# First layer of an attention and two-layer mixture-of-experts kernel: another split of the low-part work over VectorE and GpSimd, and another place for the score products

## The chip, the cores and the metric

One core of a Trainium2 chip runs the whole kernel. The metric is the device time of one execution in microseconds (us). Before the change the median of three runs is 1040.11 us (1038.76 to 1040.56). The profile is of one further execution of its own.

## What is computed

An attention with softmax over q's last axis and k's sequence axis (8 batches, 8 heads, 576 rows, 64 columns) gives 4608 tokens of 512 columns. Two expert layers follow. Each token goes to the one of 8 experts with the largest score; in layer 1 only tokens with a positive skip score are computed, the others pass through.

```python
for e in range(E):                       # layer 1, only where x @ w_skip > 0
    h = np.maximum(xc[mask] @ w1[e], 0.0)
    y[mask] = gate_w[mask, None] * (h @ w2[e])
out[do_compute] = xc + y
...
xn = x / norm(x); en = emb / norm(emb)   # layer 2, all tokens
expert_idx = argmax(xn @ en.T / tau)
out[mask] = gate_w[mask, None] * (np.maximum(x[mask] @ w1[e], 0.0) @ w2[e])
```

w1[e] is 512 x 1024, w2[e] is 1024 x 512.

## The kernel before

**High and low parts.** Every fp32 factor of a large product is used as a high part (rounded by ScalarE) and a low part (the rest), and a product is three matmuls: high by high, high by low, low by high. `hilo` (L513) makes the two parts of activations: ScalarE copies the high part out of PSUM, VectorE subtracts. `split` (L499) does the same for one expert's weights, w1 (r=0) or w2 (r=1), in 8 pieces of 128 x 512: `f` runs over 4 pairs of pieces, ScalarE writes each high part (L507), and VectorE or GpSimd writes the low part (L508), as the letter of the string `lo` says ('V' or 'P').

**Steps and blocks.** Tokens of a layer are sorted into areas by expert and worked in steps of up to two blocks of 128 tokens. A step with two blocks runs `L1two` (first product: 8 groups f of 12 matmuls, 256 tokens wide, two groups to one of the four PSUM tiles P4; after each odd f ScalarE applies the relu and VectorE takes h's low part, L541, L542), then `both` (transposes of the next step's tokens, the second of them into P4[0]), then `L2(1)` and, in the next call of `post`, `L2(0)` (second product, 24 matmuls of 512 columns each, block t into the PSUM tile py[t]). A step with one block runs `single` instead: `L1one` (24 matmuls and two relus), four groups of transposes (h in two halves, the next step's tokens in two), the four `hilo` of these, then `L2(0)`. In the run shown layer 1 has 17 steps, numbered 0 to 16; steps 2, 3, 8, 11 and 16 have one block, the other twelve two.

**Change of expert.** `change(k,r,lo)` is an `If` that splits weight r for step k where step k starts another expert, and then has SP load the expert after it (`reload`). In layer 1 steps 3, 4, 6, 9 and 12 start another expert; the w1 split stands in the `post` of the step before (letter C of the order string `seq`), the w2 split at the beginning of the step's own arm. All 8 low parts of each go to GpSimd ('PPPPPPPP').

**Layer 2's scores.** While layer 1 runs, the scores of its outputs for layer 2 are taken: `products(s,t,n)` multiplies block t of step s with the 8 rows of enB, the first n on VectorE (it reads the block's result out of py[t], L640), the other 8-n on GpSimd (it reads the copy in SBUF, L639) for ScalarE to add up (`sum`, L642). `mark`, `before` (four small matmuls) and `rank` make places of these and send the rows to the sorted X. Block 1 has all 8 products on VectorE, directly after `done(k,1)`; block 0 has 6 on VectorE and 2 on GpSimd, at the very beginning of the next step's `body` (`'pre': 'PV'`), ahead of `L1two` or `single`.

**Orders written by hand.** Each engine runs its instructions in the order of the program; nothing reorders them. `post(k)` runs L2(0) and then the letters of `seq` ('RGCMED': rank, gates, change of w1, mark, done and products of block 1, done of block 0), then gathers rows for step k+4. `body(k)` has `post(k-1)` and then the step's arm. The tail (`tail`) goes over to layer 2: it runs the first transposes of layer 2, the last `post`, the products of the last block, the w2 split, and then the first step of layer 2 in `begin`, with `one` (sum and mark) before group f1=4 of its `L1two` and `two` (total, rank, the plan's heads and rows, padding of X) before group f2=7.

**The start** (`start`): transposes of step 0, the count of tokens by expert (`total`), `split(0)` in the order VPVPVPVP with the plan's `heads` and `rows` between its pieces, padding of X and the load of enB by SP, `split(1)` in the order VPVPVPVP, then `begin`.

Of the kernel before, what the change touches and what calls it, by code (L numbers as in the profile page):

```python
# [472 lines left out]
class Moe:  # L473


    def __init__(self,tc,nc,sb,ps,cst,plan,raw,X,out,second,enD,accE,GE,ring,flags):
# [10 lines left out]
        self.enB,=st("enB",[128,8,512]); self.jk,self.ja=st("jk",[128,512],BF,2); self.pr=st("pr",[128,512],n=8-PRM["nd"])  # L487
# [11 lines left out]
    def split(self,r,mid=(),lo='VP'*4):  # L499

        nc=self.nc; H,L=self.hl[r]; n=0
        for f in range(4):
            if 0<f<=len(mid): mid[f-1]()
# [53 lines left out]
    def single(self,s):  # L557
# [78 lines left out]
    def products(self,s,t,n=8,eng='VP'):  # L636

        x=self.g(s)[:,t,0:512]
        for e in range(n,8) if 'P' in eng else (): self.nc.gpsimd.tensor_tensor(out=self.pr[e-n],in0=x,in1=self.enB[:,e],op=ALU.mult)  # L639
        for e in range(n) if 'V' in eng else (): self.nc.vector.scalar_tensor_tensor(out=self.jk,in0=self.py[t],scalar=1.0,in1=self.enB[:,e],op0=ALU.mult,op1=ALU.mult,accum_out=self.l2[s%2][:,t,e:e+1])  # L640
    def sum(self,s,t,n):
        for e in range(n,8): self.nc.scalar.activation(out=self.ja,in_=self.pr[e-n],func=AF.Copy,accum_out=self.l2[s%2][:,t,e:e+1])  # L642
# [70 lines left out]
    def layer(self,first,ws,after,kmin,gdeps=()):  # L713
# [8 lines left out]
        def change(k,r,lo='VP'*4):  # L722
            if k>=NST: return
            with tc.If(self.val(1,k)>0):  # L724
                self.split(r,(),lo)
                reload(k,r)
        def start():
            self.fresh()
            if first:
# [8 lines left out]
                with c.Else(): plan.rest(first); self.late(first,ws)  # L738
# [6 lines left out]
            self.done(0,0,first); self.val(3,1)  # L745
        def body(k):
# [7 lines left out]
            def sum():  # L754
                if first: self.sum(k-1,0,PRM['nd'])
            F=dict(P=lambda: self.products(k-1,0,PRM['nd'],'P'),V=lambda: self.products(k-1,0,PRM['nd'],'V'),M=lambda: self.mark(k-1),S=sum)
# [3 lines left out]
            if not B['chg']: change(k,1,B['lo'][0])  # L760
# [11 lines left out]
        def post(k):  # L772
# [11 lines left out]
            F=dict(C=lambda: change(k+1,0,B['lo'][2]),M=lambda: self.mark(k-1),S=lambda: self.sum(k-1,0,PRM['nd']),R=R,G=G,E=D1,D=lambda: self.done(k,0,first))  # L784
            for x in B['seq']: F[x]()
            gather(k+4)
            if k%2 and k+1<NST and not first: self.sums(k+1,2)
        def tail(k):
            if not first: post(k-1); return
# [3 lines left out]
            def one(): self.sum(k-1,0,n); self.mark(k-1)  # L793
# [6 lines left out]
            with tc.If(self.early(False,ALL)>0) as c:  # L800
                self.both(0,self.P4[1]); post(k-1); self.products(k-1,0,n); self.split(1,(),PRM['lot'])
                self.begin(False,{PRM['f1']:one,PRM['f2']:two},two if PRM['f2']==8 else None)
            with c.Else():
                post(k-1); self.split(1); self.products(k-1,0,n); one(); two(); plan.rest(False); self.late(False,after)
# [15 lines left out]
PRM={'nt': 6, 'lot': 'PPPPPPPP', 'f0': 6, 'f1': 4, 'f2': 7, 'nd': 6, 'sum': 6, 'bef': 5, 'chg': 1, 'lo': ['PPPPPPPP', 'PPPPPPPP', 'PPPPPPPP'], 'pre': 'PV', 'seq': 'RGCMED', 'early': 6, 'step': 14.514, 'win': 0.1, 'fine': {0: 2, 7: 2, 3: 2, 2: 2, 4: 2, 1: 2, 5: 2, 6: 2}, 'bufs': {'eq': 3, 'ek': 2, 'kt': 2, 'qt': 2, 'vp': 3, 'vt': 2, 'xb': 2}, 'kV': (1, 3, 7), 'qV': (), 'nA': (2, 3, 5), 'off': {'k': -12.612, 'v': 53.868, 'q': 30.476, 'K': 5.621, 'O': 26.55, 'S': 50.0}, 'tail': (6, 7), 'ob': {'v5': -85.388, 'v7': -18.189, 'q3': 3.525, 'S4': -39.842, 'v4': 49.0, 'k2': -20.193, 'v0': -57.765, 'q7': 7.453, 'k1': -50.913, 'q2': -16.574, 'K4': -7.68, 'O0': -28.323, 'v1': -80.086, 'k0': -78.46, 'q6': -32.531, 'S5': -23.128, 'K0': -77.087, 'v2': 43.27, 'K7': 21.272, 'S2': -15.874, 'k4': 14.156, 'K6': -16.911, 'v6': 32.148, 'O7': 57.371, 'S7': -5.118, 'O6': 53.378, 'K5': -39.633, 'S3': -23.995, 'q1': -13.481, 'S0': 2.649, 'O2': -14.143, 'k7': 29.483, 'q0': -9.813, 'S6': 18.001, 'q4': -35.591, 'S1': -22.407, 'k3': 2.681, 'K3': -62.071, 'O4': 17.684, 'k5': 10.878, 'q5': 2.694, 'K1': -34.335, 'O5': 18.815, 'K2': -14.953, 'v3': 36.47, 'k6': 37.121, 'O1': -10.351, 'O3': -3.795}}  # L820
# [41 lines left out]
```

## Time and profile before

| | us |
|---|---|
| median of the runs | 1040.11 |
| profiled execution, own time | 1045.66 |
| its span, first to last instruction | 1043.9 |
| attention (first matmul of layer 1 at) | 0 to 171.6 |
| layer 1, first matmul of step 0 to first matmul of layer 2 | 171.6 to 565.05 |
| layer 2, to the end of the span | 565.05 to 1043.9 |
| PE busy, share of the span | 92% |
| DVE, ACT, POOL busy | 57%, 44%, 39% |

PE is TensorE's matmul queue, DVE VectorE, ACT ScalarE, POOL GpSimd, SP the queue that issues most transfers. A timeline row has start, duration, engine, line and operation, output and inputs, shape, and in brackets the idle time before it with what released it. Matmuls overlap, so the distance of two starts tells more than a duration.

### The profile page before, as it was taken

Reading aid. Unit: us, or ns where it says so; the run is one execution under the profiler, and the core shown is the slowest. Engines: PE = TensorE matmul, PEld = TensorE weight load, DVE = VectorE, ACT = ScalarE, POOL = GpSimd, SP = SyncE. Lnnn points to the kernel's source line nnn. Section 1 sums busy time; section 2 is a strip of 40 time slices with the busy share of each in tenths; the row PEclk is TensorE's granted clock in tenths of the full one; section 3 lists DMA queues with packets and bytes.
Section 4 is the critical chain, followed back from the end, with each engine's and each line's share of the span. In section 5 each row is a group of like instructions: output and inputs, shape, how many; then the busy total and the mean of one; then the engine's idle time right before and its main releaser. Section 6 shows DMA issues by size and latency. Waiting matters only on the chain. (4 is left out here: it accounts for less than half of the span.)

```text
span 1043.9 us, 19789 instructions
## 1 busy us (share of the span) xinstructions
PE 958.6 (92%) x6075; PEld 854.5 (82%) x6075; DVE 593.0 (57%) x1576; ACT 458.8 (44%) x914; POOL 410.3 (39%) x363
## 2 busy tenths in 40 slices
PE   2988996898899999999998899999999999999994
PEld 2988885785799887779987799889898899998893
DVE  5788987874477766757775522361723423255371
ACT  5787734136343261432225423353625332455352
POOL 5487747109937174291125600041402300134040
PEclk9999997998999999999998899999999999999997
DMA  9998646634525224252111381061432610063400
GB/s 297 327 316 285 205 158 220 221 111 164 206 74 204 64 82 167 81 178 86 44 45 46 137 273 60 22 235 33 153 110 79 216 43 22 22 220 119 169 32 22
DMA packets 88632, 144.72 MB, mean 139 GB/s; under 512 B 23439, under 2 KB 48015, under 8 KB 88288
## 3 DMA queue, kind: packets, MB, share of 16 engines
q1 hardware_dynamic: 78528, 115.42, 33.8%
q0 software_dynamic: 8640, 26.61, 6.8%
q8 instruction: 74, 1.21, 0.5%
q14 instruction: 142, 1.16, 0.4%
q10 hardware_dynamic: 1248, 0.32, 0.1%
HBM read 111.08 MB, written 33.68 MB: 139 GB/s over the span
## 5 line engine op out<-in xcount | busy, mean ns | idle before, releaser
L538 PE MATMUL P<-xT,w1h 128*128 128x256 f32 x1856 | 341.6, 286 | 5.5 <-ACTq L724 2.2
L568 PE MATMUL py<-w2h,hT 128*128 128x512 f32 x1072 | 344.8, 397 | 0.3
L538 PEld LDWEIGHTS P<-xT,w1h 128*128 128x128 f32 x1856 | 294.8, 194 | 8.7 <-issue 4.2
L538 PE MATMUL P<-xT,w1l 128*128 128x256 f32 x928 | 266.0, 287 | 4.5 <-POOL w1l L508 4.2
L568 PEld LDWEIGHTS py<-w2h,hT 128*128 128x128 f32 x1072 | 202.6, 190 | 45.6 <-DVE hT L515 3.7
L568 PE MATMUL py<-w2l,hT 128*128 128x512 f32 x536 | 212.3, 396 | 4.6 <-POOL w2l L508 3.5
L542 DVE SCALAR_TENSOR_TENSOR hT<-P,hT 128x512 fp32r<-128x512 f32 x116 | 77.5, 687 | 210.2 <-ACT hT L541 210.1
L538 PEld LDWEIGHTS P<-xT,w1l 128*128 128x128 f32 x928 | 180.3, 194 | 6.3 <-POOL w1l L508 5.5
L580 POOL DMA_INDIRECT out_dram<-y,idt x38 | 38.6, 1017 | 286.5 <-ACT y L579 234.9
L640 DVE SCALAR_TENSOR_TENSOR jk<-py,enB 128x512 bf16<-128x512 f32 x198 | 136.9, 691 | 24.3 <-ACT xb L576 10.7
L541 ACT ACTIVATE hT<-P 128x512 fp32r<-128x512 f32 x116 | 67.9, 596 | 171.1 <-PE P L538 167.9
L568 PEld LDWEIGHTS py<-w2l,hT 128*128 128x128 f32 x536 | 101.5, 189 | 32.7 <-POOL w2l L508 11.2
L508 POOL TENSOR_TENSOR w1l<-kt,w1h 128x512 fp32r<-128x512 f32 x64 | 84.3, 1351 | 64.4 <-ACT w1h L507 64.2
L508 POOL TENSOR_TENSOR w2l<-vt,w2h 128x512 fp32r<-128x512 f32 x76 | 103.1, 1386 | 1.3 <-issue 0.7
L579 ACT ACTIVATE y<-py,gate 128x512 f32<-128x512 f32 x38 | 26.0, 688 | 117.5 <-PE py L568 111.3
L507 ACT CAST w2h<-vt 128x512 fp32r<-128x512 f32 x104 | 55.5, 616 | 5.8 <-issue 4.3
L507 ACT CAST w1h<-kt 128x512 fp32r<-128x512 f32 x104 | 55.7, 636 | 0.5 <-DMA xb<-X 0.5
L576 ACT COPY xb<-py 128x512 f32<-128x512 f32 x17 | 10.0, 587 | 96.3 <-DVE flag L651 50.0
L515 DVE TENSOR_TENSOR hT<-P,hT 128x512 fp32r<-128x512 f32 x18 | 12.4, 686 | 64.7 <-ACT hT L514 64.7
L639 POOL TENSOR_TENSOR pr<-xb,enB 128x512 f32<-128x512 f32 x20 | 25.4, 1291 | 60.0 <-ACT xb L576 60.0
L550 PE MATMUL P<-w1h,xT 128*128 128x512 f32 x144 | 48.2, 407 | 0.7 <-issue 0.7
L220 PE MATMUL p<-vp,ek 128*128 128x130 f32 x320 | 43.9, 291 | 3.5 <-ACT ek L210 2.6
(243 smaller groups left out, 1301.3 us busy)
## 6 DMA issues: line engine op xcount, KB each, us to landing
vt<-in_moe_w_dram SPq DMA_DIRECT2D x26, 1024.0 KB
kt<-in_moe_w_dram SPq DMA_DIRECT2D x26, 1024.0 KB
xb<-X SPq DMA_DIRECT2D x56, 266.0 KB
kt<-in_k_dram SPq DMA_DIRECT2D x16, 512.0 KB
vt<-in_v_dram SPq DMA_DIRECT2D x16, 512.0 KB
qt<-in_q_dram SPq DMA_DIRECT2D x8, 1024.0 KB
xg<-X SPq DMA_DIRECT2D x28, 266.0 KB
X<-empty SPq DMA_DIRECT2D x16, 266.0 KB
```

The source lines that it names most:

```text
L220: for j in range(NS): T.matmul(o,lhsT=ek.tile[:,j,2*c:2*c+2].rearrange(hd),rhs=vp.tile[:,2*c:2*c+2,j],start=j==0,stop=j==NB)
L507: nc.scalar.copy(h,a)
L508: (nc.gpsimd if lo[2*f+i]=='P' else nc.vector).tensor_tensor(out=l,in0=a,in1=h.bitcast(F32),op=ALU.subtract)
L538: T.matmul(o,lhsT=w[:,c,128*f:128*f+128],rhs=x[:,c],start=n==0,stop=n==11); n+=1
L541: A.activation(out=h,in_=q,func=AF.Relu)
L542: V.scalar_tensor_tensor(out=hl[:,f-1:f+1],in0=q,scalar=0.0,in1=h.bitcast(F32),op0=ALU.max,op1=ALU.subtract)
L550: T.matmul(self.P4[f],lhsT=x[:,c,0:128],rhs=w[:,c,512*f:512*f+512],start=n==0,stop=n==11); n+=1
L568: T.matmul(self.py[t],lhsT=x[:,c,a],rhs=w[:,c],start=n==0,stop=n==23); n+=1
L579: A.activation(out=y,in_=p,func=AF.Copy,scale=gt)
L580: P.indirect_dma_start(out=self.out,out_offset=IO(self.idt[:,i:i+1]),in_=y,in_offset=None,bounds_check=NTOK-1,oob_is_err=False)
L639: for e in range(n,8) if 'P' in eng else (): self.nc.gpsimd.tensor_tensor(out=self.pr[e-n],in0=x,in1=self.enB[:,e],op=ALU.mult)
L640: for e in range(n) if 'V' in eng else (): self.nc.vector.scalar_tensor_tensor(out=self.jk,in0=self.py[t],scalar=1.0,in1=self.enB[:,e],op0 ...
```

## The change

In layer 1 the low parts of w1 at a change of expert go to VectorE (all 8), those of w2 stay on GpSimd. At the start all of w1's go to VectorE, with the plan's heads and rows behind them, and all of w2's to GpSimd, in two halves: pairs 0 and 1 ahead of `begin`, pairs 2 and 3 inside its first product. Both blocks now have 6 products on VectorE and 2 on GpSimd (four tiles `pr` in place of two). GpSimd's follow the w2 split; ScalarE's sums of both blocks stand behind `both`. VectorE's products of block 0 move from ahead of the first product to behind the first low part of h in `L1two`; in a step of one block they, `before` and the sums move from ahead of `single` to behind it. In such a step the w2 split is made in halves, pairs 0 and 1 ahead of `single`, pairs 2 and 3 between its second and third `hilo`. The last `post` has another order ('GCRMED'), keeps w1 on GpSimd and all 8 products on VectorE; `one` moves to group 1 and `two` behind the first product.

```diff
-    def split(self,r,mid=(),lo='VP'*4):
+    def split(self,r,lo='VP'*4,part=range(4)):
...
-        for f in range(4):
-            if 0<f<=len(mid): mid[f-1]()
+        for f in part:
...
-        h(); x(); g(); y()
+        h(); x(); mid(); g(); y()
...
-        for e in range(n,8) if 'P' in eng else (): self.nc.gpsimd.tensor_tensor(out=self.pr[e-n],in0=x,in1=self.enB[:,e],op=ALU.mult)
+        for e in range(n,8) if 'P' in eng else (): self.nc.gpsimd.tensor_tensor(out=self.pr[(8-n)*t+e-n],in0=x,in1=self.enB[:,e],op=ALU.mult)
...
-                self.split(0,(lambda: plan.heads(cst['base0'][:,0:8]),lambda: plan.rows(8*AREA,0,5)))
+                self.split(0,'V'*8); plan.heads(cst['base0'][:,0:8]); plan.rows(8*AREA,0,5)
...
-                self.split(1)
-                with tc.If(early>0) as c: self.begin(first)
+                def w2(*f): return lambda: self.split(1,'P'*8,f)
+                w2(0,1)()
+                with tc.If(early>0) as c: self.begin(first,{2:w2(2),4:w2(3)})
...
-                if first: self.products(0,1)
+                if first: self.products(0,1,PRM['nd'],'V')
...
-            if first:
-                for x in B['pre']: F[x]()
-            def arm(c): return lambda: [x() for w,x in ((B['sum'],sum),(B['bef'],before)) if w==c]
+            def P():
+                if first: [self.products(k-1,t,PRM['nd'],'P') for t in range(2)]
+            def V():
+                if first: self.products(k-1,0,PRM['nd'],'V')
+            def arm(c): return lambda: [x() for w,x in ((2,V),(B['sum'],sum),(B['bef'],before)) if w==c]
             with tc.If(two>0) as c:
                 if B['chg']: change(k,1,B['lo'][0])
+                P()
                 self.L1two({f:arm(f) for f in range(8)})
                 self.both(k+1,self.P4[0])
                 arm(8)()
                 self.L2(1)
             with c.Else():
-                if B['chg']: change(k,1,B['lo'][1])
-                for f in range(8): arm(f)()
-                self.single(k)
-                arm(8)()
+                change(k,1,B['lo'][1],(0,1))
+                self.single(k,lambda: change(k,1,B['lo'][1],(2,3)))
+                P()
+                for f in range(9): arm(f)()
...
+            nd,seq,lo=(PRM['nt'],PRM['seqt'],PRM['lot']) if last and first else (PRM['nd'],B['seq'],B['lo'][2])
...
-                    if first: self.products(k,1)
+                    if first: self.products(k,1,nd,'V')
...
-                self.both(0,self.P4[1]); post(k-1); self.products(k-1,0,n); self.split(1,(),PRM['lot'])
+                self.both(0,self.P4[1]); post(k-1,True); self.products(k-1,1,n,'P'); self.products(k-1,0,n); self.split(1,PRM['lot'])
```

In the table of constants of layer 1: `nt` 6 to 8, `seqt` 'GCRMED' (new), `f1` 4 to 1, `f2` 7 to 8, `sum` 6 to 8, the third string of `lo` 'PPPPPPPP' to 'VVVVVVVV'; `'pre': 'PV'` is gone.

## Rows read from the trace of the kernel before

**Rows 1.** Stretches of 25 us: length, busy PE, PEld, DVE, ACT, POOL, clock, DMA.

```profile
225.00:250.00 25.00, 21.34 (x91) 16.55 (x91) 15.22 (x47) 14.89 (x31) 16.54 (x14) 0.86 0.16 50
...
325.00:350.00 25.00, 25.00 (x170) 23.02 (x169) 18.14 (x54) 7.24 (x18) 11.30 (x10) 1.00 0.46 158
```

**Rows 2.** Timeline of PE, first matmul of steps 3 to 6, 8 to 10.

```profile
238.59 0.47 PE L550 MATMUL P<-w1h,xT 128*128 128x512 f32 x1
...
261.32 0.47 PE L538 MATMUL P<-xT,w1h 128*128 128x256 f32 x2 [0.16 <-issue]
...
291.49 0.40 PE L538 MATMUL P<-xT,w1h 128*128 128x256 f32 x2
...
315.17 0.40 PE L538 MATMUL P<-xT,w1h 128*128 128x256 f32 x2
...
362.80 0.47 PE L550 MATMUL P<-w1h,xT 128*128 128x512 f32 x1
...
377.10 0.40 PE L538 MATMUL P<-xT,w1h 128*128 128x256 f32 x2
...
405.45 0.40 PE L538 MATMUL P<-xT,w1h 128*128 128x256 f32 x2
```

**Rows 3.** Timeline of PE, first matmul of step 3 that reads a low part.

```profile
241.81 0.79 PE L550 MATMUL P<-w1l,xT 128*128 128x512 f32 x1 [2.74 <-POOL w1l L508]
```

**Rows 4.** Waits of the whole span: who for whom, us in total, times, longest.

```profile
PEld py L568 <- POOL w2l L508: 11.2, 17, 0.7
```

**Rows 5.** Stretches behind waits of PE: length, busy PE, PE clock, DMA share, GB/s.

```profile
241.80:247.70 5.90, 5.89 (x14) 0.51 0.00 0
...
556.00:561.60 5.60, 5.58 (x17) 0.50 0.00 1
...
264.20:268.00 3.80, 3.80 (x18) 0.56 0.70 257
...
577.40:582.00 4.60, 4.58 (x30) 0.64 0.10 40
...
198.40:200.40 2.00, 0.01 (x1) 1.00 0.85 244
```

**Rows 6.** Timeline of PE, transposes and second product of step 2.

```profile
229.60 0.60 PE L527 MATMUL pxT<-ident,xb 128*128 128x128 f32 x4
...
231.05 0.66 PE L555 MATMUL P<-ident,h 128*128 128x128 f32 x4 [0.85 <-ACT h L551]
...
232.38 0.50 PE L568 MATMUL py<-w2h,hT 128*128 128x512 f32 x1
```

**Rows 7.** Timeline of DVE: step 2's last low part; six products, first and last.

```profile
234.24 0.68 DVE L515 TENSOR_TENSOR xT<-P,xT 128x512 fp32r<-128x512 f32 x1
...
239.91 0.69 DVE L640 SCALAR_TENSOR_TENSOR jk<-py,enB 128x512 bf16<-128x512 f32 x1 [0.65 <-ACT xb L576]
...
243.58 0.69 DVE L640 SCALAR_TENSOR_TENSOR jk<-py,enB 128x512 bf16<-128x512 f32 x1
```

**Rows 8.** Timeline of PE, second transposes of the first step.

```profile
186.83 0.66 PE L527 MATMUL P<-ident,GE 128*128 128x128 f32 x4 [0.92 <-DVE hT L542]
```

**Rows 9.** Timeline of PE, change of layers: transposes, layer 2's first product, count.

```profile
556.02 1.09 PE L527 MATMUL pxT<-ident,GE 128*128 128x128 f32 x4 [4.16 <-issue]
...
565.05 0.40 PE L538 MATMUL P<-xT,w1h 128*128 128x256 f32 x2
...
577.41 0.17 PE L496 MATMUL pm<-oh,ones 128*1 128x8 bf16 x1 [2.14 <-DVE oh L670]
```

**Rows 10.** Timeline of ACT, eight high parts of w2 in step 9.

```profile
379.21 4.26 ACT L507 CAST w2h<-vt 128x512 fp32r<-128x512 f32 x8 [0.53 <-issue]
```

**Rows 11.** Low parts of weights, L508: min/median/max ns, first and last start.

```profile
L508 POOL TENSOR_TENSOR w2l<-vt,w2h x76: 1251/1286/1778, 177.7 to 1013.4; 128x512 fp32r<-128x512 f32 x76
...
L508 DVE TENSOR_TENSOR w1l<-kt,w1h x40: 669/683/1790, 171.7 to 1002.2; 128x512 fp32r<-128x512 f32 x40
```

**Rows 12.** ACT's sums of GpSimd's products, L642: min/median/max ns.

```profile
L642 ACT ACTIVATE jk<-pr x34: 622/630/632, 209.8 to 575.2; 128x512 bf16<-128x512 f32 x34
```

More of the change, by code (lines that the diff above doesn't have):

```diff
@@ L498, in total @@
         self.nc.vector.tensor_copy(self.plan.cnt,p)
[L499 to L503 removed]
+    def split(self,r,lo='VP'*4,part=range(4)):
+        nc=self.nc; H,L=self.hl[r]
+        for f in part:
             for i in range(2):
@@ L556, in Th, with single @@
         return lambda: self.hilo(p,*[t[:,4*g:4*g+4,0:128] for t in self.hT])
-    def single(self,s):
+    def single(self,s,mid):
         self.L1one()
         x,h,y,g=self.Tx(s+1,0),self.Th(0),self.Tx(s+1,1,self.P4[0]),self.Th(1)
-        h(); x(); g(); y()
+        h(); x(); mid(); g(); y()
     def L2(self,t,mid=None):
@@ L721, in reload, with change @@
                     with tc.If(nx<9): self.load(r,after[r],0)
-        def change(k,r,lo='VP'*4):
+        def change(k,r,lo='VP'*4,part=range(4)):
             if k>=NST: return
             with tc.If(self.val(1,k)>0):
-                self.split(r,(),lo)
-                reload(k,r)
+                self.split(r,lo,part)
+                if part[-1]==3: reload(k,r)
         def start():
@@ L732, in start @@
                 self.total(self.accE)
-                self.split(0,(lambda: plan.heads(cst['base0'][:,0:8]),lambda: plan.rows(8*AREA,0,5)))
+                self.split(0,'V'*8); plan.heads(cst['base0'][:,0:8]); plan.rows(8*AREA,0,5)
                 self.arrange(first,gdeps)
                 nc.sync.dma_start(out=self.enB.rearrange('p e d -> p (e d)'),in_=self.enD.rearrange('e d -> (e d)').unsqueeze(0).to_broadcast([128,4096]))
-                self.split(1)
-                with tc.If(early>0) as c: self.begin(first)
-                with c.Else(): plan.rest(first); self.late(first,ws)
+                def w2(*f): return lambda: self.split(1,'P'*8,f)
+                w2(0,1)()
+                with tc.If(early>0) as c: self.begin(first,{2:w2(2),4:w2(3)})
+                with c.Else(): w2(2,3)(); plan.rest(first); self.late(first,ws)
             for s in (2,3,4): gather(s)
@@ L743, in start, with sums @@
                 self.done(0,1,first)
-                if first: self.products(0,1)
+                if first: self.products(0,1,PRM['nd'],'V')
             self.done(0,0,first); self.val(3,1)
+        def sums(k,n):
+            for t in range(2): self.sum(k,t,n)
         def body(k):
@@ L754, in sum @@
             def sum():
-                if first: self.sum(k-1,0,PRM['nd'])
-            F=dict(P=lambda: self.products(k-1,0,PRM['nd'],'P'),V=lambda: self.products(k-1,0,PRM['nd'],'V'),M=lambda: self.mark(k-1),S=sum)
-            if first:
-                for x in B['pre']: F[x]()
-            def arm(c): return lambda: [x() for w,x in ((B['sum'],sum),(B['bef'],before)) if w==c]
-            if not B['chg']: change(k,1,B['lo'][0])
+                if first: sums(k-1,PRM['nd'])
+            def P():
[3 more added lines that the diff above has]
+            def arm(c): return lambda: [x() for w,x in ((2,V),(B['sum'],sum),(B['bef'],before)) if w==c]
             with tc.If(two>0) as c:
                 if B['chg']: change(k,1,B['lo'][0])
+                P()
                 self.L1two({f:arm(f) for f in range(8)})
@@ L783, in G @@
                 if k%2==0: self.gates(k,2,first)
-            F=dict(C=lambda: change(k+1,0,B['lo'][2]),M=lambda: self.mark(k-1),S=lambda: self.sum(k-1,0,PRM['nd']),R=R,G=G,E=D1,D=lambda: self.done(k,0,first))
-            for x in B['seq']: F[x]()
+            F=dict(C=lambda: change(k+1,0,lo),M=lambda: self.mark(k-1),R=R,G=G,E=D1,D=lambda: self.done(k,0,first))
+            for x in seq: F[x]()
             gather(k+4)
@@ L788, in tail @@
         def tail(k):
-            if not first: post(k-1); return
+            if not first: post(k-1,True); return
             if k==0:
@@ L792, in tail, with one @@
             n=PRM['nt']
-            def one(): self.sum(k-1,0,n); self.mark(k-1)
+            def one(): sums(k-1,n); self.mark(k-1)
             def two():
@@ L800, in tail @@
             with tc.If(self.early(False,ALL)>0) as c:
-                self.both(0,self.P4[1]); post(k-1); self.products(k-1,0,n); self.split(1,(),PRM['lot'])
+                self.both(0,self.P4[1]); post(k-1,True); self.products(k-1,1,n,'P'); self.products(k-1,0,n); self.split(1,PRM['lot'])
                 self.begin(False,{PRM['f1']:one,PRM['f2']:two},two if PRM['f2']==8 else None)
             with c.Else():
-                post(k-1); self.split(1); self.products(k-1,0,n); one(); two(); plan.rest(False); self.late(False,after)
+                post(k-1,True); self.split(1); self.products(k-1,1,n,'P'); self.products(k-1,0,n); one(); two(); plan.rest(False); self.late(False,after)
         twos={}
```

8 lines of the change are left out of this document (4 added, 4 removed).

## The prediction

> **What bounds the kernel now.** I read first the stretches of 25 us, then the timeline of TensorE by steps, then what ended its waits. In most of layer 1 TensorE is the bound: a quiet stretch has it busy for all of its 25.0 us at full clock, while one with steps of one block and changes of expert shows 21.3 us and a clock of 0.86 [rows 1]. So the steps are compared by their first matmuls. A plain step of two blocks lasts 315.17 - 291.49 = 23.7 us, step 8 (one block) 14.3, step 9 (another expert) 28.4, step 4 (another expert) 30.2, step 3 (one block, another expert) 22.7 [rows 2]. Steps 11 and 12 repeat 8 and 9 within 0.1 us. What is above 23.7 in steps 4, 9 and 12 is 6.5 + 4.7 + 4.7 us, and its releaser is GpSimd, which makes w1's eight low parts and only then w2's: step 3 waits 2.74 us for w1's [rows 3], the second products wait in 17 pieces for w2's [rows 4]. Behind four of TensorE's waits the granted clock stands at 0.51, 0.50, 0.56 and 0.64 for 5.9, 5.6, 3.8 and 4.6 us, near the lower of its two levels (1.2 of 2.4 GHz); one idle stretch of 2.0 us stands at 1.00 [rows 5]. Lost behind the four are (1 - clock) x length: 2.9, 2.8, 1.7 and 1.7 us, 2.3 in the mean.
>
> **Steps of one block: the products get in front of the second product.** In step 2 the transposes start at 229.60 and the second product at 232.38, 2.8 us later, 0.85 of it a wait for ScalarE [rows 6]. VectorE's six products of the block before are over by then, since they stand ahead of `single`. In the new order they stand behind its last low part. They read py[0] in PSUM, and the second product, L2(0), is the next thing to write py[0]: it has to wait for the last of them. VectorE ends the last low part at 234.24 + 0.68 = 234.9 [rows 7], about 0.9 earlier if ScalarE's wait goes with the sums, so 4.4 us behind the start of the transposes. Six products take 243.58 + 0.69 + 0.08 - 239.91 = 4.4 us [rows 7]. With 0.2 us to TensorE the second product starts 9.0 us behind the transposes in place of 2.8: +6.2 us, an idle time of over 6 us. A wait of TensorE for VectorE to leave a PSUM tile does occur in the old trace (0.92 us for P4[0] [rows 8]); for py it does not, since the products were always early. I add 2.3 us for the clock (bounds 0 and 2.9 [rows 5]): **+8.5 us** in each of steps 2, 8 and 11, +25.5.
>
> Step 16 has the same order, but there TensorE waits 4.16 us at the change of layers anyway [rows 9], and the products run beside it: 0 (without that cover +8.5).
>
> Step 3 also splits w2. Its second half puts four copies on ScalarE (half of 4.26 us [rows 10]) ahead of h's second half, so the products end about 2 us later: two products of TensorE (14.3 - 2.8 = 11.5), a gap of 11.0, and 2.3 for the clock give 24.8 in place of 22.7: **+2.1**. The stall on w1 that it has today is saved in this.
>
> **Changes of expert.** VectorE takes 0.68 us for a low part at the median where GpSimd takes about 1.29 [rows 11]: eight in 5.4 us, while L2(0) of a step of one block, with its slow clock, lasts some 8. GpSimd is then free for w2 as soon as ScalarE has copied: 8 x 1.29 = 10.3 us within the first product (about half of a step's 23.7). Steps 4, 9 and 12 come down to a plain 23.7: **-15.9** (upper bound: all that they have above it; lower: 0, if another queue is late).
>
> Step 6 follows a step of two blocks and pays today nothing for its change. In the new order VectorE does rank, eight low parts and `mark` ahead of done of block 1. ScalarE starts w1's copies behind four sums (0.63 each and a read of the accumulator, some 3.3 us [rows 12]), so the low parts end about 10 us behind the start of step 5's second product. Then come on VectorE and ScalarE `mark` 1.4, done of block 1 0.8, its copy 0.6, six products 4.4, done of block 0 0.8, its copy 0.6 (estimates from such pieces of step 5): 18.6, that is 7.6 behind the 11.0 of the second product. ScalarE's copies of w2 (4.3 [rows 10]) are queued ahead of the relus, so h's first low part is there at 7.6 + 4.3 + 1.4 = 13.3 of step 6, where the transposes into P4[0] want it at 12.1: 1.2 us. Another 4.4 us of products and 0.7 later comes its second low part, at 18.4, where the second product, begun at 13.9, wants it at 15.6: some 2.7 us. With 1.7 for the clock [rows 5]: **+5.6** (bounds 0 and 7).
>
> **Start and change of layers.** At the start VectorE is rid of w2's low parts, so the 0.92 us wait goes: **-0.9** [rows 8]. The plan's heads now follow eight low parts, so SP's eight paddings and the load of enB come some 6 us later; the first products may wait for enB, with VectorE's room ahead of `both` as cover: 0 (without it up to +2). SP's gathers still wait for the plan's later rows, as now. At the change of layers `mark` no longer waits for GpSimd's products behind w1's split. The 2.14 us [rows 9] go, and the 1.7 us of slow clock behind them [rows 5]: **-3.8**. The count then stands behind the first product, where TensorE has the transposes to do, and the scatters on GpSimd come no later than now.
>
> **At nothing:** two more products on GpSimd and two sums on ScalarE in each plain step (2.6 and 1.6 us), beside an idle GpSimd and behind `both`; without that cover `mark` comes some 0.3 us late. VectorE is relieved of 1.5 us a step that never reached TensorE. The second `If` for w2 in steps without a change and the loads of weights on SP: 0 to +1 in all. Layer 2 keeps its orders.
>
> **Sum:** 25.5 + 2.1 - 15.9 + 5.6 - 0.9 - 3.8 = +12.6 us. The profiled execution took 1045.66 us, 5.6 above the median of the runs (1040.11), and would take 1058.3; on the median it is **1052.7 us**.
>
> **Rivals.**
> - *Faster: the products do not hold L2(0).* VectorE is idle between done of the block before and the low parts of h. If the products run in that time, as they do today, every gap stays closed. Then steps 2, 8 and 11 lose even the 0.85 wait [rows 6] (-2.6), step 3 comes to about 17 us under GpSimd's pace (-5.7), and with -15.9, -0.9 and -3.8 and no backlog in step 6 it is -28.9: 1011 us. It decides where the second product of step 2 starts under 4 us behind its transposes. Against it: the program's order on VectorE. Chance 0.07.
> - *No change: the clock holds.* The gaps come, but cost no half speed: 4 x 2.3 + 1.7 less, and a little less in step 6: about 1041. For it: the idle stretch at 1.00. Against it: the four others [rows 5]. Chance 0.12.
> - *Slower still: VectorE's split is slowed by GpSimd.* Old low parts of w1 on VectorE run up to 1.79 us where GpSimd subtracts beside them [rows 11]. At 1.1 us, an estimate between median and maximum, each split is 3.4 us longer; what of it TensorE sees lies between 0 and 5 x 3.4, and I take half, 8.5: 1061 us. Against it: GpSimd has no subtractions at most of these times. Chance 0.13. The Trainium skill (GPSIMD Engine Reference, section 1, Specifications) says that GpSimd's way to SBUF contends with VectorE instructions that have two SBUF inputs; the low parts are such, the products and h's low parts, with an input in PSUM, are not. By that rule the trace agrees: 0.68 alone, 1.79 at worst beside GpSimd.
>
> **Numbers.** The forecast has 0.64, its own range 1045 to 1060; 0.04 is left for what I don't see. A measurement of this kernel can tell about 0.2%, 2.1 us, from no change. The case of the holding clock reaches from 1035 to 1046 and gives 0.05 to faster, 0.04 to the same, 0.03 to slower; the unheld products give 0.07 to faster; the forecast gives 0.02 to the same and 0.62 to slower, the slowed split 0.13 to slower, the unknown 0.01, 0.02 and 0.01. The range from 1040 to 1063 leaves out the unheld products, the lower part of the holding clock and the worst of the slowed split.
>
> **What would show it.** Right: in steps 2, 3, 8 and 11 the first matmul of py stands 9 to 11 us behind the transposes, released by VectorE's products, with a clock near 0.5 behind it; steps 4, 9, 12 at 23.7; w1's low parts on VectorE near 0.68 us; a wait of 2 to 3 us in step 6's second product; no wait of the count. The forecast is wrong if those gaps are under 3 us, if the clock stays at 1.00 behind them, or if steps 4, 9 and 12 keep over 2 us of their excess.

## The result, and the profile after

The changed kernel takes 1051.26 us (median of four runs, 1050.05 to 1051.72); the kernel before takes 1040.34 beside it (four runs, 1038.76 to 1041.74). The ratio is 1.0104, 95% interval 1.0086 to 1.0121: slower by 10.9 us, where 12.6 was forecast. The profiled execution took 1051.72, its span is 1050.0.

The two spans can't be subtracted as they stand: the attention, which the change does not touch, ended 6.1 us earlier in the second one (first matmul of step 0 at 165.53, before at 171.60). From that matmul to the end it is 884.5 us, before 872.3: +12.2. The steps show where it lies. Each number is the distance of two first matmuls in the timeline of TensorE; the columns behind "after" are the experiments A to I below, and row 17 is layer 2's first step.

```
step     before  after    A      B      C      D      E      F      G      H      I
2         14.52  22.37  13.62  19.65  22.04  22.04  22.04  13.63  13.58  13.57  13.57
3         22.73  24.04  24.38  23.89  24.40  23.87  23.84  24.57  18.44  23.36  18.93
4         30.17  23.67  28.15  25.25  24.16  23.68  23.67  26.35  31.83  23.77  29.02
6         23.66  29.10  30.42  29.10  24.28  29.06  27.90  24.19  25.42  25.42  27.67
8         14.30  22.48  14.50  19.66  21.53  22.43  21.34  15.61  16.82  16.88  16.88
9         28.35  23.66  26.30  23.93  23.66  23.65  23.66  24.66  23.66  23.67  23.66
11        14.25  21.91  16.69  19.87  21.35  21.85  21.30  15.88  16.28  17.75  17.62
12        28.36  23.67  24.04  23.65  23.67  23.65  23.65  23.84  24.01  23.65  23.66
16        21.71  21.94  19.01  21.32  21.70  21.96  21.67  19.30  19.31  20.76  19.77
17        30.31  30.83  30.97  30.66  30.01  36.07  31.25  29.27  31.54  30.68  30.41
```

Timeline of TensorE in the changed kernel: transposes, second product and next step of step 2 (rows 6 and 2 before), the second product of step 3, the two waits of step 6, and layer 2's second step.

```profile
222.34 0.60 PE L526 MATMUL pxT<-ident,xb 128*128 128x128 f32 x4
...
231.01 0.76 PE L567 MATMUL py<-w2h,hT 128*128 128x512 f32 x1 [6.50 <-DVE cl L686]
...
239.27 0.39 PE L549 MATMUL P<-w1h,xT 128*128 128x512 f32 x1
...
255.16 0.76 PE L567 MATMUL py<-w2h,hT 128*128 128x512 f32 x1 [8.28 <-DVE cl L686]
...
325.67 1.12 PE L526 MATMUL P<-ident,xb 128*128 128x128 f32 x4 [2.54 <-DVE hT L541]
...
330.55 0.50 PE L567 MATMUL py<-w2h,hT 128*128 128x512 f32 x1 [0.84 <-DVE hT L541]
...
602.61 0.80 PE L537 MATMUL P<-xT,w1h 128*128 128x256 f32 x2 [6.57 <-ACTq L723]
```

In step 2 the second product now starts 8.7 us behind the transposes, 6.5 of them idle; before it was 2.8 [rows 6]. The last row is the wait that nobody forecast; it stood at 2.2 before. Its releaser, ACTq L723, is ScalarE's own sequencer (not its compute part) at the branch of `change`.

Timeline of VectorE beside that wait: step 2's last low part, its first and last product, and what follows.

```profile
225.91 0.68 DVE L514 TENSOR_TENSOR xT<-P,xT 128x512 fp32r<-128x512 f32 x1
226.51 0.68 DVE L639 SCALAR_TENSOR_TENSOR jk<-py,enB 128x512 bf16<-128x512 f32 x1
...
230.17 0.69 DVE L639 SCALAR_TENSOR_TENSOR jk<-py,enB 128x512 bf16<-128x512 f32 x1
230.78 0.08 DVE L639 DVE_READ_ACCUMULATOR jk<-py,enB 128x1 f32 x1
230.78 0.17 DVE L686 TENSOR_TENSOR cl<-pm,oh 128x16 f32<-128x16 f32 x1
```

The last product reads py[0] until 230.86, and TensorE writes py[0] from 231.01. The wait is put down to `rank`'s small multiplication (L686), which starts in the same moment as the last product's closing read (230.78); run A decides between the two.

VectorE's first and second low part of h in step 6, whose first matmul is at 310.65, and TensorE's wait in step 16:

```profile
324.92 0.69 DVE L541 SCALAR_TENSOR_TENSOR hT<-P,hT 128x512 fp32r<-128x512 f32 x1 [5.82 <-ACT hT L540]
...
329.80 1.88 DVE L541 SCALAR_TENSOR_TENSOR hT<-P,hT 128x512 fp32r<-128x512 f32 x3
```

```profile
563.18 1.08 PE L526 MATMUL pxT<-ident,GE 128*128 128x128 f32 x4 [5.73 <-DVE jk L639]
```

Stretches of the changed kernel (length, busy PE, PEld, DVE, ACT, POOL, clock, DMA): the first as in [rows 1], the others the second products of steps 2, 3, 8 and 11.

```profile
225.00:250.00 25.00, 15.87 (x68) 12.98 (x68) 15.28 (x40) 15.71 (x34) 9.87 (x9) 0.80 0.41 148
...
231.00:239.30 8.30, 8.29 (x25) 6.59 (x26) 6.89 (x20) 2.01 (x4) 2.37 (x2) 0.65 0.38 116
255.10:263.30 8.20, 8.13 (x24) 6.52 (x25) 5.18 (x13) 6.15 (x14) 4.65 (x4) 0.66 0.40 155
377.50:385.90 8.40, 8.37 (x24) 6.72 (x25) 7.11 (x22) 2.03 (x4) 2.10 (x2) 0.64 0.32 99
447.50:455.20 7.70, 7.62 (x25) 6.16 (x26) 6.59 (x20) 1.96 (x4) 2.06 (x2) 0.72 0.35 106
```

TensorE is idle for some 5.5 us more of the first stretch than before (15.87 busy in place of 21.34; the stretch holds work that came some 7 us later before, so this is a rough comparison). The four second products run at a mean granted clock of 0.64 to 0.72, so at the lower level (1.2 of 2.4 GHz) for a good part.

Low parts of weights in layer 1 of the changed kernel, L507 (ns min/median/max, first and last start; rows 11 before):

```profile
L507 DVE TENSOR_TENSOR w1l<-kt,w1h x48: 669/684/726, 165.6 to 452.6; 128x512 fp32r<-128x512 f32 x48
L507 POOL TENSOR_TENSOR w2l<-vt,w2h x48: 1260/1292/1993, 169.7 to 466.8; 128x512 fp32r<-128x512 f32 x48
```

VectorE's low parts were not slowed: 726 ns at the most.

### The profile page after: what moved, and what is told of

Its sections match the earlier page's. It is cut to its first block, busy times and chain, and to the rows that moved or that the text cites. A ratio compares the mean times of both kernels' runs of the same rounds, so it can differ in the third digit from the quotient of the medians.

```text
span 1050.0 us, 19892 instructions
## 1 busy us (share of the span) xinstructions
PE 951.4 (91%) x6075; PEld 859.7 (82%) x6075; DVE 595.4 (57%) x1572; ACT 480.6 (46%) x974; POOL 397.8 (38%) x353
## 5 line engine op out<-in xcount | busy, mean ns | idle before, releaser
L567 PE MATMUL py<-w2h,hT 128*128 128x512 f32 x1072 | 351.3, 404 | 30.1 <-DVE cl L686 27.8
L567 PEld LDWEIGHTS py<-w2h,hT 128*128 128x128 f32 x1072 | 208.2, 194 | 75.5 <-ACT w1h L506 19.7
L639 DVE SCALAR_TENSOR_TENSOR jk<-py,enB 128x512 bf16<-128x512 f32 x176 | 121.5, 690 | 13.7 <-ACT xb L575 4.6
L507 POOL TENSOR_TENSOR w2l<-vt,w2h 128x512 fp32r<-128x512 f32 x80 | 107.8, 1383 | 52.4 <-ACT w2h L506 44.5
L567 PEld LDWEIGHTS py<-w2l,hT 128*128 128x128 f32 x536 | 104.6, 195 | 21.1
L638 POOL TENSOR_TENSOR pr<-xb,enB 128x512 f32<-128x512 f32 x40 | 50.3, 1290 | 48.6 <-ACT xb L575 48.6
L507 DVE TENSOR_TENSOR w1l<-kt,w1h 128x512 fp32r<-128x512 f32 x84 | 64.8, 837 | 3.7 <-ACT w1h L506 3.4
L507 POOL TENSOR_TENSOR w1l<-kt,w1h 128x512 fp32r<-128x512 f32 x20 | 28.9, 1465 | 67.6 <-ACT w1h L506 60.4
L641 ACT ACTIVATE jk<-pr 128x512 bf16<-128x512 f32 x64 | 40.6, 634 | 22.9 <-POOL pr L638 19.8
```

The costliest lines, as they stand in the source:

```text
L507: (nc.gpsimd if lo[2*f+i]=='P' else nc.vector).tensor_tensor(out=l,in0=a,in1=h.bitcast(F32),op=ALU.subtract)
L567: T.matmul(self.py[t],lhsT=x[:,c,a],rhs=w[:,c],start=n==0,stop=n==23); n+=1
```

## The experiments

Ratios are to the kernel before on the same chip (1043.9 to 1045.5 us there). First the changed kernel again, run beside E, F and G.

> The changed kernel again, unchanged, as the base for the other kernels of this call on their chip: 1.008 to 1.011 of the kernel before, with the step durations of its first profile (22.4, 24.0, 22.5 and 21.9 us in steps 2, 3, 8 and 11; 29.1 in step 6) within 0.5 us. Step 1 can be 1.5 us longer, as in the four kernels before, if the granted clock is again low at its beginning.

Measured: 1059.11 us, 1.0122 (1.0094 to 1.0150). The steps were not within 0.5 us of the first profile: 21.1, 23.4, 21.2 and 22.8 us in steps 2, 3, 8 and 11, and 30.7 in step 6 (its second wait was 2.38 us there, not 0.84); step 1 was 1.5 us longer. The waits for py were the same (6.51, 8.28, 6.51 and 6.51 us), but the second products behind them took 7.0, 7.5, 7.1 and 8.4 us, where they had taken 8.3, 8.1, 8.4 and 7.6: how long the clock stays low is not the same in each execution. So below, a difference of about 1 us in a step with such a wait, or of 1.5 in step 1, tells nothing by itself.

**A. Products ahead again in steps of one block.**

```diff
-                change(k,1,B['lo'][1],(0,1))
+                V(); change(k,1,B['lo'][1],(0,1))
...
-                for f in range(9): arm(f)()
+                for f in range(9):
+                    if f!=2: arm(f)()
```

> In steps of one block VectorE's six products of the block before go back ahead of the w2 split and of `single`; all else as in the changed kernel. Theory (the products hold py, and so L2(0)): the second product of steps 2, 8 and 11 starts some 2 us behind its transposes in place of 8.7, at a granted clock near 1.00, and these steps last 13.3 to 14.3 us in place of 22. But the w1 change that follows now has only a short L2(0) beside it: steps 4, 9 and 12 rise from 23.7 to 28 to 33 us. Net about -12, near 1039 us. Rival (the profile names VectorE's small multiplication of `rank` as releaser of that wait, not the products, so that the order of the products is not the cause): the gaps stay at 8.7 us and the time at 1051 us.

Measured: 1044.71 us, 0.9996 (0.9984 to 1.0007). Timeline of TensorE: step 2's transposes and second product, the first matmul of step 4; and the stretch of that second product.

```profile
230.24 0.27 PE L526 MATMUL pxT<-ident,xb 128*128 128x128 f32 x1
...
232.48 0.50 PE L567 MATMUL py<-w2h,hT 128*128 128x512 f32 x1
...
262.79 0.58 PE L537 MATMUL P<-xT,w1h 128*128 128x256 f32 x1 [5.30 <-ACT w1h L506]
```

```profile
232.40:238.40 6.00, 5.75 (x25) 4.45 (x25) 3.87 (x12) 5.62 (x15) 2.02 (x2) 1.00 0.20 71
```

The gap is 2.2 us and the clock 1.00. One reordering on VectorE takes back 22.0 of the 23.7 us that steps 2, 8 and 11 had lost: the products' hold on py[0] is shown to be the cause there, and the named releaser was only the next instruction. In step 11 a wait of 1.6 us for the products and a clock of 0.77 are left (16.69 us, expected at most 14.3). Step 16 falls too, from 21.94 to 19.01. Step 3 does not (24.38): its gap shrinks from 10.4 to 6.6 us, but then step 4's first matmul waits 5.3 us for w1's high part, so a second limit lay beside the products. Step 4 rises as expected (28.2), step 9 less (26.3), step 12 hardly (24.04); step 11's second product, still 7.2 us long, may have been its cover, which no run tests.

**B. TensorE kept busy in the gap.** 26 matmuls of 512 columns, whose result nothing reads, are added in steps 2, 3, 8 and 11.

```diff
+                if first and k<16:
+                    for i in range(26): nc.tensor.matmul(self.P4[1],lhsT=self.hT[0][:,0,0:128],rhs=self.hl[1][0][:,0],start=True,stop=True)
```

> Behind `single` in steps 2, 3, 8 and 11 TensorE gets 26 more matmuls of 512 columns whose result nothing reads, so that it works through most of the wait for py (26 x 0.234 = 6.1 us of 6.5). Theory (the slow second product behind the wait is the granted clock, and the clock falls because TensorE stood idle): L2(0) of these steps takes about 5.7 us in place of 7.7 to 8.5 at a granted clock near 1.00, so 2 to 2.9 us less in each of three steps and somewhat less in step 3 (its wait is longer than the added matmuls): -7 to -10, 1041 to 1044 us. Rival (L2(0) is slow for its own operands or its pace through py, not for the clock): the step durations stay at 21.9 to 22.5 and 24.0 us and the time at 1051 us, or above by what the added matmuls delay.

Measured: 1055.21 us, 1.0094 (1.0077 to 1.0110). The second products of steps 2 and 3, timeline and stretches:

```profile
237.98 0.47 PE L567 MATMUL py<-w2h,hT 128*128 128x512 f32 x1 [0.49 <-DVE cl L686]
...
260.27 0.63 PE L567 MATMUL py<-w2h,hT 128*128 128x512 f32 x1 [2.29 <-DVE cl L686]
```

```profile
238.00:243.50 5.50, 5.50 (x24) 4.56 (x25) 5.20 (x13) 2.01 (x4) 2.37 (x2) 1.00 0.28 102
260.30:267.40 7.10, 7.10 (x24) 5.69 (x25) 3.42 (x9) 5.66 (x13) 5.26 (x5) 0.76 0.54 211
```

Where 0.5 us of idleness is left, L2(0) takes 5.5 us at a clock of 1.00; where 2.3 us are left, 7.1 at 0.76. So the slow second product is the clock, and the idleness ahead of it brings it. The time itself did not follow, where -7 to -10 us were expected: 1.0094 against 1.0104 and 1.0122 is inside the intervals. Steps 2, 8 and 11 gave 7.6 us by the table, but step 4 took 1.6 back (a wait of 1.3 for h's low part, which the late start had probably covered), step 1 another 1.5 and the steps behind layer 2's first another 2.1, which no part of this edit touches.

**C. w1's low parts back on GpSimd.**

```diff
-... 'lo': ['PPPPPPPP', 'PPPPPPPP', 'VVVVVVVV'], ...
+... 'lo': ['PPPPPPPP', 'PPPPPPPP', 'PPPPPPPP'], ...
```

> Layer 1's w1 low parts at changes of expert go back to GpSimd, all else as changed. Theory (the backlog on VectorE in step 5 makes step 6 late, and the products alone make the gaps in steps of one block): step 6 falls from 29.1 to some 24 us (-5.4), the gaps of 8.7 us in steps 2, 8 and 11 stay, steps 4, 9 and 12 rise by 0 to 2 us each because w2's low parts come behind w1's on GpSimd but L2(0) with its wait and slow clock covers most; in all 1046 to 1049 us. Rival (VectorE's w1 low parts bring most of what steps 4, 9 and 12 gained and cost step 6 little): steps 4, 9 and 12 go back up by 4 to 6 us each, step 6 by 0 to 1 down, 1060 to 1066 us.

Measured: 1054.07 us, 1.0080 (1.0064 to 1.0097). Step 6 falls to 24.28, the gaps stay, steps 4, 9 and 12 stay within 0.5 of 23.7. The theory holds: where the step ahead has its long gap, GpSimd is in time for these steps too, and VectorE's split costs 4.8 us in step 6. It is not all cost: without it steps 5 and 7 rise by some 1 us each (waits of 0.7 and 0.9 for h's low part).

**D. The change of layers as before.**

```diff
-PRM={'nt': 8, 'seqt': 'GCRMED', 'lot': 'PPPPPPPP', 'f0': 6, 'f1': 1, 'f2': 8, ...
+PRM={'nt': 6, 'seqt': 'RGCMED', 'lot': 'PPPPPPPP', 'f0': 6, 'f1': 4, 'f2': 7, ...
```

> The change of layers goes back to the parameters of before (order RGCMED, 6 products of the last block on VectorE and 2 on GpSimd, sum and mark before group 4, total and plan before group 7), all else as changed. Theory (VectorE's plan for layer 2 and the gathers behind it set when layer 2's next step starts, so TensorE's waits ahead of it are cover): layer 2's second step starts 30.3 to 30.9 us behind layer 2's first matmul, as in both kernels, and the time stays within 1.5 us of 1051. Rival (my forecast's term: the removed wait of the count and its slow clock were worth 3.8 us, and something else took them back): 3 to 4 us slower, 1054 to 1055 us.

Measured: 1063.17 us, 1.0157 (1.0139 to 1.0175); 36.07 us for layer 2's first step. My expectation fell. TensorE's wait of the count (us in total, times, longest), and GpSimd's timeline:

```profile
PE pm L496 <- DVE oh L669: 6.8, 1, 6.8
```

```profile
578.92 10.05 POOL L507 TENSOR_TENSOR w1l<-kt,w1h 128x512 fp32r<-128x512 f32 x8
588.94 4.96 POOL L638 TENSOR_TENSOR pr<-xg,enB 128x512 f32<-128x512 f32 x4
```

Both blocks now have products on GpSimd, four in place of two, and they stand behind w1's split; `mark` waits for them, and the count for `mark`: 6.8 us in place of 2.14 [rows 9]. So the new order at the change of layers is worth 5.2 us in this step (3.6 to the end of the span), but only against a load that the change itself brought.

**J. The new change of layers alone, on the kernel before** (the same constants, and `seqt` in the last `post`).

> The kernel before with the new change of layers alone (order GCRMED in the last post, 8 products of block 0 on VectorE, sum and mark before group 1, total and plan behind the first product of layer 2). My forecast's term: -3.8 us, 0.9963 of the kernel before, with layer 2's second step 26.5 us behind its first matmul in place of 30.3. Theory now (VectorE's plan for layer 2 ends later or no earlier, and the values read behind it set the second step's start): the wait of the count goes and TensorE is some 3.5 us earlier at the end of its second products, but the wait for layer 2's values grows from 2.2 to some 6 us; the second step starts 29.5 to 31 us behind the first matmul, and the time is within 1.5 us of before (0.9985 to 1.0015). A rival on the other side: the later plan costs more than the count's wait, 1.002 or above.

Measured: 1044.96 us, 1.0005 (0.9990 to 1.0020). What TensorE waited for at the change of layers: first in this run, then in the kernel after (columns: us in total, times, longest).

```profile
PE P L538 <- ACTq L724: 5.4, 1, 5.4
PE P L538 <- DVEq L724: 1.5, 1, 1.5
```

```profile
PE P L537 <- ACTq L723: 6.6, 1, 6.6
PE pxT L526 <- DVE jk L639: 5.7, 1, 5.7
```

The end of VectorE's plan in this run, then in the kernel after, with ScalarE's next instruction there:

```profile
590.51 0.17 DVE L468 CAST pl_ctl<-pl_ee 1x24 int32<-1x24 f32 x1
```

```profile
595.95 0.17 DVE L468 CAST pl_ctl<-pl_ee 1x24 int32<-1x24 f32 x1
...
596.43 0.30 ACT L631 ACTIVATE ex<-GE,ri 128x8 f32<-128x8 f32 x1 [4.88 <-DVE ri L630]
```

The count's wait is gone, and the second products of layer 2's first step end 24.2 us behind its first matmul in place of 28.1. But the next step needs the values that VectorE's plan writes last (L468, at 590.51 here, 24.2 behind that first matmul; 25.0 in the kernel before), and the wait for them grows from 2.2 to 5.4 + 1.5 us: the step is 0.65 us shorter (29.66), the one behind it 2.5 longer (27.75). The theory holds: the 3.8 us went into this wait. In the thirteen profiles the next step starts 4.4 to 7.1 us behind the start of L468 (5.3 before the change, 6.7 after it). What those microseconds consist of was not tried: besides the values that are read, ScalarE's exponentials of layer 2's gates (L631) stand ahead of its branch, and they wait for an instruction of VectorE right behind the plan. No run moves the plan alone, so which of the two holds the step is open; both come behind the plan.

**E. Products of block 0 later in steps of two blocks.**

```diff
-... for w,x in ((2,V), ...
+... for w,x in ((6,V), ...
```

> In steps of two blocks VectorE's six products of block 0 move from behind h's first low part to behind its third (group 2 to group 6 of the first product); all else as changed, steps of one block too. Theory (step 6 is late by VectorE's whole backlog, eight low parts, mark, done and products of block 1, of which the products of block 0 are only the last): the wait of 2.5 us for P4[0] becomes shorter by at most 1, the second wait of 0.84 goes, step 6 falls from 29.1 to between 26.5 and 28.5; -0.5 to -2.5 us in all. Rival (block 0's products alone make step 6 late, as they make the steps of one block late): step 6 falls to 24, -5 us.

Measured: 1056.41 us, 1.0101 (1.0076 to 1.0125). Step 6 takes 27.90 us; the 0.84 is gone, the first wait stays (2.53 us). Of the 5.4 us that step 6 had lost 1.2 come back, of the 7.0 us in the changed kernel's second profile 2.8. The theory holds: the backlog ahead makes step 6 late, and block 0's products are the lesser part of it.

**F. By kind of step:** A and E, and w1's low parts to VectorE behind steps of one block, to GpSimd behind steps of two.

```diff
+            def C():
+                if not first or last: change(k+1,0,lo); return
+                with tc.If(two>0) as c: change(k+1,0,'P'*8)
+                with c.Else(): change(k+1,0,'V'*8)
```

> Three parts together, on the kernel with the products ahead in steps of one block: there the products stand ahead of `single`; in steps of two blocks they stand behind h's third low part; and w1's low parts go to VectorE behind a step of one block, to GpSimd behind one of two. Theory (VectorE's queue, by what stands ahead of h's low parts, sets each of the lost stretches): the waits of 1.1 us in step 4, 2.5 and 1.2 us in step 6 and 2.3 us in step 9 that were left with the products ahead in steps of one block go, with the slow clock behind them: step 6 from 30.4 to some 24.3, step 9 from 26.3 to 23.7, step 4 from 28.2 to about 25; about -11 us against that kernel, 0.988 to 0.992 of the kernel before. Rival (the products only move the wait: h's last low part is then late by 4.4 us and the second product waits for it in each step of two blocks): 0.998 to 1.01 of before.

Measured: 1037.53 us, 0.9931 (0.9910 to 0.9953): faster than both kernels. Step 6 falls to 24.19, step 9 to 24.66 (0.7 us of its wait is left), step 4 to 26.35; against A step 8 rises by 1.1 and step 11 falls by 0.8. That is 0.65% below A, some 7 us in place of 11: the waits named went or shrank; step 6 gave the 6.2 us expected of it, steps 4 and 9 gave 1.8 and 1.6 where 3.2 and 2.6 were expected. The three parts were not tried one by one on A.

**G. ScalarE's sums behind w1's copies** in steps of one block, on F.

```diff
                 with c.Else():
                     change(k+1,0,'V'*8)
+                    sums(k-1,PRM['nd'])
...
-                    if f!=6: arm(f)()
+                    if f not in (6,8): arm(f)()
```

The last `post` gets the same sums in an `If` of its own, not shown.

> As the kernel before it in this call, and in steps of one block ScalarE's four sums stand behind its copies of the next w1 instead of ahead of them. Theory (step 4's first matmul waits 5.3 us for w1's high part because ScalarE's queue holds the copies behind sums that wait for GpSimd, whose four products stand behind the w2 split): that wait goes, step 3 falls from some 24 to 19 us, step 4 loses its slow clock (23.7); -5 to -8 us against the kernel before it, 0.982 to 0.986 of the kernel before the change. Rival (the load of w1 or its low parts end that wait, not the copies): step 3 stays within 1 us.

Measured: 1035.25 us, 0.9902 (0.9876 to 0.9927), the lowest median of all. Step 3 falls to 18.44 as expected, but step 4 rises to 31.83, and steps 6 and 8 by 1.2 each. Low parts of w1 behind step 3, GpSimd's products beside them, and TensorE's wait:

```profile
L507 DVE TENSOR_TENSOR w1l<-kt,w1h x8: 677/1720/1771, 254.4 to 264.0; 128x512 fp32r<-128x512 f32 x8
```

```profile
255.53 6.76 POOL L638 TENSOR_TENSOR pr<-xb,enB 128x512 f32<-128x512 f32 x4
```

```profile
262.39 0.58 PE L537 MATMUL P<-xT,w1l 128*128 128x256 f32 x1 [5.12 <-POOLq L797]
```

Two things that had been apart now meet. VectorE's low parts take 1.72 us each beside GpSimd's products, and these 1.69 (6.76 / 4) in place of 1.24. And TensorE waits 5.1 us for GpSimd, which has no part in this split, to pass the branch at L797 (POOLq is GpSimd's sequencer; L797 is the `If` whose other arm gives w1's low parts to GpSimd).

**H. GpSimd's products ahead of its w2 low parts** in steps of one block, on G.

```diff
-                V(); change(k,1,B['lo'][1],(0,1))
+                P(); V(); change(k,1,B['lo'][1],(0,1))
...
-                P()
```

> As the kernel with the sums behind w1's copies, and in steps of one block GpSimd's four products stand ahead of its w2 low parts instead of behind them. In that kernel step 4 had taken 31.8 us: TensorE waited 5.1 us behind its second matmul, until GpSimd had ended its products and passed the branch that splits w1, and VectorE's eight low parts took 10.2 us beside GpSimd's products in place of 4.9. Theory (GpSimd comes to that branch late because its products follow w2's low parts, and its products slow VectorE's): with the products first, GpSimd passes the branch when w2's low parts end, 10.3 us behind the products' end, some 261 us into the span; L2(0) of step 3 goes at their pace and ends then, so step 3 rises to 22 to 23 us, step 4 falls to 23.7 to 25; -4 us against that kernel, 0.984 to 0.988 of the kernel before. VectorE's w1 low parts stay slow (beside w2's), but nothing waits for them. Rival (only the slow low parts on VectorE held step 4): they are slow here too, and step 4 stays above 29 us.

Measured: 1035.66 us, 0.9918 (0.9886 to 0.9950). Step 4 is at 23.77 and step 3 at 23.36, so 3.1 us less for both, though VectorE's low parts are still slow (maximum 1766 ns). The expected -4 us against G do not show in the time: step 16 takes 1.5 us back (20.76 against 19.31), and step 11 another 1.5: behind the same idle stretch of 2.17 us the clock of its second product was 1.00 in G and 0.79 here (stretches of G, then of H):

```profile
436.30:442.00 5.70, 5.70 (x26) 4.74 (x27) 5.14 (x13) 5.42 (x14) 2.26 (x2) 1.00 0.16 63
```

```profile
432.10:439.20 7.10, 7.10 (x26) 5.74 (x27) 6.54 (x16) 6.00 (x15) 2.25 (x2) 0.79 0.20 79
```

**I. w1's low parts always on VectorE**, on G: the branch by kind goes, the sums keep theirs.

```diff
-                with tc.If(two>0) as c: change(k+1,0,'P'*8)
-                with c.Else():
-                    change(k+1,0,'V'*8)
-                    sums(k-1,PRM['nd'])
+                change(k+1,0,'V'*8)
+                with tc.If(two>0) as c: change(NST,0)
+                with c.Else(): sums(k-1,PRM['nd'])
```

> As the kernel with the sums behind w1's copies, but w1's low parts go to VectorE in every change, so that GpSimd has no part in the branch that splits w1. Theory (TensorE's 5.1 us in step 4 were a wait for GpSimd to pass a branch in which it may write w1's low part, not for VectorE's slow low parts): that wait falls below 1.5 us though VectorE's low parts still take 9 to 10 us beside GpSimd's products; step 4 24 to 27 us; step 6 has VectorE's backlog again, 27 to 28.5 us in place of 25.4. In all -2 to -5 us against that kernel. Rival (the slow low parts themselves): the wait of 5 us and step 4's 31 us stay, step 6 adds 2 to 3 us.

Measured: 1036.60 us, 0.9926 (0.9900 to 0.9952). First matmul of step 4 that reads a low part, and VectorE's low parts:

```profile
257.63 0.47 PE L537 MATMUL P<-xT,w1h 128*128 128x256 f32 x2 [0.43 <-issue]
257.94 0.28 PE L537 MATMUL P<-xT,w1l 128*128 128x256 f32 x1
```

```profile
L507 DVE TENSOR_TENSOR w1l<-kt,w1h x8: 677/1762/1782, 254.6 to 264.3; 128x512 fp32r<-128x512 f32 x8
```

The low parts are as slow as in G, and the wait of 5.1 us is gone: it was the branch. Step 4 stays long all the same (29.02, expected 24 to 27): a wait of 2.5 us for h's low part follows in it (VectorE's queue has the slow low parts until 264.9 us and `mark` behind them), so they probably cost something after all, by another path; no run tests it. The four kernels F to I lie within 0.3% of each other and their intervals overlap.

## Why the prediction was right, and where it was not

| step of the prediction | forecast | measured (table; after minus before) |
|---|---|---|
| steps 2, 8, 11: products hold py[0] | +25.5 | +7.8 +8.2 +7.7 = +23.7 |
| step 3 | +2.1 | +1.3 |
| steps 4, 9, 12: w1 on VectorE | -15.9 | -6.5 -4.7 -4.7 = -15.9 |
| step 6: backlog | +5.6 | +5.4 |
| step 16 under its cover | 0 | +0.2 (by luck, see below) |
| start (step 0) | -0.9 | -0.8 |
| change of layers | -3.8 | +0.5 |
| all else | 0 to +1 | -2.3 (steps 1, 7, 10, 15 by 0.3 each; behind layer 2's first step 1.1) |

**How close the sum is.** The profiled executions differ by 12.2 us from layer 1's first matmul on, the forecast was 12.6. The sum is better than its terms: the change of layers came out 4.3 us above its term, and the products (1.8), step 3 (0.8) and what was put at nothing (some 2.3) came out below theirs. That they cancel is luck.

**Right: the products in steps 2, 8 and 11.** A shows the cause, B the clock's share. The gap is 8.7 us in steps 2 and 8 and 8.9 in step 11, not 9.0, and the second product lasts 8.26 in step 2 where it lasted 6.21 before (each from its first matmul to the next step's), 2.05 more in place of 2.3. This part is not steady: it is 2.4 and 1.6 in steps 8 and 11, and 0.8, 1.1 and 2.5 in the second profile of the same kernel.

**Right in the number, with a limit overlooked: step 3.** The gap is 10.4, not 11.0, and the step 0.5 us shorter than forecast. But A closes a part of this gap and the step stays at 24.4: ScalarE copies the next w1 only behind sums that wait for GpSimd, whose products stand behind the w2 split. With the sums behind the copies as well the step is 18.4 (G). The forecast had only the products.

**Right by luck: step 16.** The products are not free there. TensorE waits for them at the change of layers (5.73 us, where 4.16 had been), and with the products ahead the step takes 19.0 us (A), 2.9 less. In A the step is 2.7 us shorter than before the change (the 0.86 us of wait for h is gone, the wait at the change of layers is 3.40, and the clock behind it is 0.86 in place of 0.73). In the changed kernel the two happen to cancel.

**Right in the sum, with another reason: the changes of expert.** Steps 4, 9 and 12 came down to 23.7 as forecast. C shows that VectorE's speed was not needed for it: with the long gap, GpSimd is in time too. With the gap closed, steps 4 and 9 are at 28.2 and 26.3 even with VectorE (A).

**Right in the sum: step 6.** C shows the cause, VectorE's eight low parts. h's first low part was put at 13.3 us of the step and stands at 324.92 - 310.65 = 14.3, the second at 18.4 and stands at 19.2. The two waits came as 2.54 and 0.84, not 1.2 and 2.7.

**The step that failed: the change of layers.** "The 2.14 us go, and the 1.7 us of slow clock behind them: -3.8." Both went, but I had not asked what ends last behind them. What stands behind VectorE's plan does (J): layer 2's second step starts only behind its values and gates, 4.4 to 7.1 us behind the start of the plan's last instruction in every profile. In the old order TensorE waited only 2.2 us for it, so nearly all of the 3.8 us became a longer wait: the term measured +0.5 in place of -3.8. I had also costed two more products on GpSimd at nothing; at this place that holds only with the new order (D, 5.2 us in that step).

**The rivals.** "The products do not hold L2(0)" and "the clock holds" fell by the rows of the result and by B. The slowed split did not happen in the change, since behind step 3 ScalarE's sums held w1's copies until GpSimd's products were over; G took the sums away, and there it is: 1.72 us each. That bears out the row the rival was priced by (1.79 [rows 11]). The Trainium skill (SBUF — State Buffer, section Summary: rules for kernel authors) says that of a VectorE instruction with two SBUF inputs and a GpSimd one that reads SBUF the second to issue waits until the first is done. G agrees nearly: VectorE's and GpSimd's pieces come in turn, one of each per 1.7 us, where alone they take 0.61 (4.91 us for eight in the changed kernel) and 1.24, 1.85 together, so a little of it overlaps.

## What to carry to other kernels

When an instruction moves back in its queue, ask first which tile it reads and who writes that tile next: here six cheap products, moved into idle time of their own engine, kept TensorE out of one PSUM tile for 6.5 us. Price a removed wait only up to the next thing that ends last, and look for it by name (here the plan on VectorE). Where one fix closes a gap, look at what the gap was covering: A and G each moved part of their gain into the next step.

## What the runs showed of the hardware

- **Idle stretches of about 2 us don't tell what the clock does.** In the stretch ahead of step 1 TensorE was idle for 1.42 us in the changed kernel, 2.0 in the kernel before, 2.10 in J (whose first steps are those of the kernel before) and 1.93 in A. In the 4 us behind it the clock was 1.00, 1.00, 0.57 and 0.63, and the first product, up to the next transposes, took 11.6, 11.6, 13.1 and 13.1 us. In step 11 the same 2.17 us gave 1.00 in G and 0.79 in H. After waits of 6.5 us and more for py the second product ran at 0.63 to 0.79 in each of the five profiles that have them (the changed kernel twice, C, D and E). That a few idle microseconds cost up to 1.5 us more in one execution and nothing in another is part of the spread of these runs.
- **A reader waited for the engine of the arm that was not taken.** With w1's low part written by GpSimd in one arm and by VectorE in the other (G), TensorE waited 5.1 us until GpSimd had passed the branch, though VectorE's arm was taken; with VectorE in every case (I) the wait was gone at the same pace of VectorE, and so it was with GpSimd at the branch earlier (H).
- **VectorE and GpSimd slow each other, and both ends show it:** 0.68 to 1.72 us on VectorE and 1.24 to 1.69 us on GpSimd for 128x512 pieces, both with two inputs in SBUF (G).
